# Pooled attention and squared-ReLU feed-forward on one core: all engine orders from an explicit table, and some loads and stores on ScalarE's DMA queue

## The chip, the cores and the metric

The kernel runs on one core of one Trainium2 chip. That core has TensorE (PE in the rows) for matrix products, VectorE (DVE), ScalarE (ACT) and GpSimd (POOL) for work on vectors, and SyncE (SP), which issues DMAs here. Each engine works through its own queue in order; semaphores join them. The metric is device time in microseconds (us), lower is better.

## The reference

Four batches of eight heads, 1152 keys of 64 numbers each. Queries are averaged in pairs, so a head has 576 of them. Attention over all keys is followed by a feed-forward layer with a squared ReLU on the 2304 x 512 result.

```python
q_pool = q.reshape(B, H, S // 2, 2, D).mean(axis=3)
scores = np.matmul(q_pool, k.transpose(0, 1, 3, 2)) / np.sqrt(D)
attn = np.exp(scores - scores.max(-1, keepdims=True))
attn = attn / (attn.sum(-1, keepdims=True) + 1e-09)
x = np.matmul(attn, v)          # then (b, s, h, d) -> (2304, 512)
r = np.maximum(x @ w_in, 0.0)   # 512 -> 2048
out = (r * r) @ w_out           # 2048 -> 512
```

All arrays are float32, and q and k come with a spread that makes scores large.

## The kernel before

The float32 products are made from float16 parts: a number is split into a high part and the low rest, and three products of parts are added. The work is a list of 2265 steps, each with a name, the engines that may do it, the steps that it depends on, and buffers that it takes and gives back. A name is two letters and numbers; these occur in the text:

- **Pairs of heads.** There are 16 (n = 0 to 15). Steps LK, LQ, LV load k, q, v of a pair into one of two `raw` buffers; KA and KD (and QA, QD, VA, VD) make the high and low parts; KT and QT transpose them by DMA into `kT` and `qT`; QX copies the halves of `qT` across partitions.
- **Chunks of 128 queries.** A pair has nine, 144 in all. S is the product with the keys, into one of two PSUM tiles `s`. MX (line 771, DVE) finds the row maximum, MB (line 778 on ACT, 781 elsewhere) finishes the bias, EX (line 795, ACT) takes the exponent. For chunks 36 to 143, HI (line 799 on ACT) casts the result to float16, LO (line 807) makes the low part, and TR (line 810) transposes both by DMA into `PT`. For chunks 0 to 35 (pairs 0 to 3) TP transposes on TensorE in float32 and TC (lines 846, 848) copies out. PV is the product with v, ED moves it out of PSUM.
- **Blocks of 256 rows.** There are nine of the feed-forward layer (j = 0 to 8). RV, RT, RU, RB and XR apply the softmax sums, XQ to XD scale and split the block; H (line 1119) and O (line 1168) are the two products in eight steps each; HA, G1, G2, G3 are the ReLU, its square and its split between them; OD and ST write the block out.
- **Weights.** w_in and w_out come through staging buffers (WL, UL, line 1222) and are turned into parts by W and U steps, of which W5 or U4, for instance, reads a staging buffer.

S of chunk i waits for EX of chunk i-2, because there are two `s` tiles. H, O, RB and other small products share two PSUM banks `ba` until the last EX; then six more (`bt`) open.

The method `Plan.order` decides engine and order. It simulates the list with fixed costs (`COST`, `Clock`), takes at each moment the step with the best priority (`off` and `off0` in `CFG`), and chooses among a step's engines by expected end. All DMAs are issued by `nc.sync`, that is by SyncE's queue, also QX of the pairs for which `CFG` says so.

Of the kernel before, what the change touches and what calls it, by code (L numbers as in the profile page):

```python
# [33 lines left out]
}  # L34


class Clock:


    W = 3413.3  # L40

    def __init__(self):
        self.warm, self.edge, self.used = False, self.W, 0.0

    def turn(self):
# [1413 lines left out]
```

## Time and profile before

| | us |
|---|---|
| median of three runs | 794.99 (794.79 to 800.12) |
| span of the profiled execution, first to last instruction | 794.4 |
| TensorE busy in it | 743.8 (94%) |
| VectorE busy | 571.4 (72%) |
| ScalarE busy | 589.7 (74%) |
| GpSimd busy | 350.1 (44%) |

The profiled execution has no time of its own beside its span; the span lies 0.6 us under the median of the runs. TensorE's busy time counts matrix products from start to modelled end, and at the lower of its two clock levels (1.2 and 2.4 GHz) the same product is busy twice as long. In a row, PEclk 1.00 is the higher level. Issuing a DMA isn't counted as busy.

### The profile page before, as it was taken

To read this page: it belongs to the slowest core of one execution; us is meant where nothing else is said; L and a number is where in the kernel's file an instruction comes from. 1 tells how busy PE (TensorE), PEld (TensorE's weight loads), DVE (VectorE), ACT (ScalarE), POOL (GpSimd) and SP (SyncE) were. 2 spreads that over 40 slices of the span, in tenths; PEclk is the share of its full clock that TensorE was granted. 3 is DMA by queue.
4 is the path that set the end of the run, shared out by engine and by line. 5 is a ranking of instruction groups with operands and counts; after the bars stand their busy time and mean duration, and the time that the engine had idled before them with its cause. 6 is when DMAs were issued, how large, how long until landed. Compare 5 with 4: busy or idle time off the path is not lost.

```text
span 794.4 us, 15338 instructions
## 1 busy us (share of the span) xinstructions
PE 743.8 (94%) x5998; PEld 491.7 (62%) x5998; DVE 571.4 (72%) x920; ACT 589.7 (74%) x874; POOL 350.1 (44%) x240
## 2 busy tenths in 40 slices
PE   5889888888999999979999999999999999999997
PEld 4665555555766676546756775577567657785654
DVE  4789987787789798787879888898898764202311
ACT  5776967899798798688987997899989864403512
POOL 2455421346686475544646575575366321001200
PEclk8899899999899999979999999999999999999999
DMA  8686573417889999999999999999999991000011
GB/s 325 225 233 187 167 204 106 120 31 142 168 172 199 194 225 218 219 206 215 186 212 199 217 208 207 202 228 195 209 217 191 173 183 25 1 2 13 14 27 28
DMA packets 324840, 128.96 MB, mean 162 GB/s; under 512 B 307104, under 2 KB 307872, under 8 KB 324768
## 3 DMA queue, kind: packets, MB, share of 16 engines
q1 hardware_dynamic: 324768, 127.98, 77.3%
q8 instruction: 47, 0.77, 0.4%
q14 instruction: 25, 0.20, 0.1%
HBM read 45.09 MB, written 4.72 MB: 63 GB/s over the span
## 4 chain that ended last, share of the span: by engine, by line
PE 78%; DVE 7%; ACT 5%; DMA 5%; issue 3%; SPq 1%; POOL 0%; DVEq 0%; ACTq 0%; POOLq 0%
PE ba L1168 17%; PE ba L1119 17%; PE s L760 12%; PE ba L955 10%; PE bt L1168 7%; PE bt L1119 6%; DVE s L771 3%; PE ba L836 3%; DMA region<-in_moe_w_in_dram 2%; PE ba L947 2%; ACT buf L795 2%; PE s L755 2%; DMA w<-in_moe_w_out_dram 2%; DVE PT L848 1%; ACT PT L846 1%
## 5 line engine op out<-in xcount | busy, mean ns | idle before, releaser
L771 DVE TENSOR_SCALAR_CACHE_REDUCE s<-s,esc 128x1152 f32<-128x1152 f32 x135 | 190.9, 1420 | 32.2 <-PE s L760 21.9
L1119 PEld LDWEIGHTS <-w 128*128 128x128 f16 x1728 | 169.4, 99 | 33.1 <-issue 7.0
L795 ACT ACTIVATE buf<-s,ca 128x1152 f32<-128x1152 f32 x144 | 174.4, 1212 | 14.2 <-DVE s L771 7.7
L807 POOL TENSOR_TENSOR buf<-buf,buf 128x1152 f16<-128x1152 f32 x53 | 130.9, 2472 | 54.1 <-ACT buf L799 44.2
L760 PE MATMUL s<-kT,qT 128*128 128x512 f16 x720 | 137.6, 330 | 9.3 <-ACT buf L795 9.0
L1168 PE MATMUL ba<-w,region 128*128 128x512 f16 x624 | 142.2, 379 | 1.3 <-ACT region L1129 0.7
L1168 PEld LDWEIGHTS <-region 128*128 128x128 f16 x864 | 82.8, 98 | 96.3 <-issue 2.5
L1119 PE MATMUL ba<-region,w 128*128 128x256 f16 x1104 | 128.7, 275 | 1.3 <-DVE x L1046 1.2
L799 ACT ACTIVATE buf<-buf 128x1152 f16<-128x1152 f32 x107 | 124.5, 1163 | 5.9 <-DMA PT<-buf 1.7
L760 PEld LDWEIGHTS <-qT 128*128 128x128 f16 x720 | 63.6, 100 | 66.9 <-issue 18.1
L807 DVE TENSOR_TENSOR buf<-buf,buf 128x1152 f16<-128x1152 f32 x55 | 77.1, 1404 | 14.4 <-ACT buf L799 14.1
L955 PE MATMUL ba<-PT,v 128*64 128x320 f16 (+1 forms) x1296 | 85.4, 290 | 0.0
L955 PEld LDWEIGHTS <-v 128*64 128x64 f16 x1296 | 70.8, 111 | 14.7 <-issue 7.1
L1146 POOL TENSOR_TENSOR region<-region 128x512 f16<-128x512 f32 x35 | 49.2, 1405 | 51.4 <-ACT region L1139 50.0
L1146 DVE TENSOR_TENSOR region<-region 128x512 f16<-128x512 f32 x37 | 29.1, 793 | 58.7 <-ACT region L1139 55.8
L836 PE MATMUL ba<-ident,buf 128*128 128x128 f32 x324 | 54.4, 296 | 14.8 <-ACT buf L795 5.5
L1134 ACT ACTIVATE region<-region 128x512 f16<-128x512 f32 x72 | 45.1, 626 | 20.3 <-PE bt L1168 17.3
L836 PEld LDWEIGHTS ba<-ident,buf 128*128 128x128 f32 x324 | 36.4, 148 | 30.7 <-ACT PT L846 8.7
L1168 PE MATMUL bt<-w,region 128*128 128x512 f16 x240 | 52.6, 379 | 0.0
L1142 POOL TENSOR_TENSOR region<-region 128x512 f32<-128x512 f32 x11 | 14.6, 1329 | 83.6 <-ACT region L1134 83.6
L846 ACT ACTIVATE PT<-ba 128x384 f32<-128x384 f32 x76 | 35.7, 490 | 18.6 <-PE ba L836 17.1
L1119 PE MATMUL bt<-region,w 128*128 128x256 f16 x432 | 48.7, 273 | 0.0
(189 smaller groups left out, 944.1 us busy)
## 6 DMA issues: line engine op xcount, KB each, us to landing
raw<-in_q_dram SPq DMA_DIRECT2D x32, 288.0 KB, 3.8
raw<-in_k_dram SPq DMA_DIRECT2D x15, 576.0 KB, 4.8
region<-in_moe_w_in_dram SPq DMA_DIRECT2D x8, 1024.0 KB, 6.2
w<-in_moe_w_out_dram SPq DMA_DIRECT2D x8, 1024.0 KB, 5.8
raw<-in_v_dram SPq DMA_DIRECT2D x12, 576.0 KB, 4.7
out_dram<-buf SPq DMA_DIRECT2D x22, 128.0 KB, 2.4
v<-in_v_dram SPq DMA_DIRECT2D x4, 576.0 KB, 6.2
out_dram<-half SPq DMA_DIRECT2D x14, 128.0 KB, 3.3
```

The costliest lines, as they stand in the source:

```text
L760: nc.tensor.matmul(s[:, x, :w], lhsT=qt[:, l].rearrange("p c m -> p (c m)")[:, 128 * c0 + h : 128 * c0 + h + 255 : 2], rhs=rhs, **st)
L771: nc.vector.tensor_scalar(st3(), st3(), sc, 3e38, op0=ALU.mult, op1=ALU.min, accum_out=a[:, x : x + 1])
L795: nc.scalar.activation(P(), st3(), AF.Exp, bias=a[:, 1:2], scale=s1, accum_out=col)
L799: nc.scalar.activation(hl()[:, 0], P(), AF.Copy)
L807: e.tensor_tensor(out=hl()[:, 1], in0=P(), in1=hl()[:, 0], op=ALU.subtract)
L836: nc.tensor.matmul(t[:, y], lhsT=P()[:, c * 128 : (c + 1) * 128], rhs=ident, is_transpose=True, start=(y == 0), stop=(y == 2), skip_group_ ...
L846: nc.scalar.activation(out, t, AF.Copy)
L955: nc.tensor.matmul(px[h * 64 : (h + 1) * 64, 64 * r * (1 - h) : 64 * r * (1 - h) + N], lhsT=vv[:, h, kc, vl, :], rhs=p2(vi, r, h, 9 * pl + ...
L1119: nc.tensor.matmul(ph[:, f2], lhsT=w16[0][:, SLOT[f // 4], wl, a, f % 4 * 128 : (f % 4 + 1) * 128], rhs=xhl()[:, xl, a], start=(i == 0), s ...
L1134: nc.scalar.activation(gt[u][:, 0], rt[u % 2], AF.Square)
L1146: e.tensor_tensor(out=gt[u][:, 1], in0=rt[u % 2], in1=gt[u][:, 0], op=ALU.subtract)
L1168: nc.tensor.matmul(p[:, :DM], lhsT=g[:, gl, f % 2, tt * 128 : (tt + 1) * 128], rhs=w16[1][:, SLOT[f // 4], wl, f % 4], start=(f == 0 and g ...
```

## The change

The simulation in `Plan.order`, its costs and its priorities go. In their place stands the string `ORDER`: three characters a step, which give the step's number, its engine and the buffer that it takes. The list of steps and their dependences stay. A sixth engine name, AQ, means a DMA issued by `nc.scalar`, that is ScalarE's queue; loads of pairs 4 to 15 and all stores may have it. The listing contains functions for another way to make the scores (`flipped`, `part`, `kz`), which are not used, since `FLIP` is empty in `CFG`.

```diff
+ORDER = (
+    "26W27W28W29X2C000W2E12DG2BO2G02F82I12H82K02MW2JG2LG81006W02803O82G01O2P18AG13W8382QG8408B904G86185807O"
...
-    ENG = ("PE", "ACT", "DVE", "POOL", "SP")
+    ENG = ("PE", "ACT", "DVE", "POOL", "SP", "AQ")
...
+        for k in range(0, len(ORDER), 3):
+            a, b, c = (DIGIT[x] for x in ORDER[k : k + 3])
+            i, e, x = 64 * a + b, self.ENG[c // 8], c % 8
             o = ops[i]
+            assert i not in gone and e in o["engs"] and all(self.at[d] in gone for d in o["deps"] + list(o["after"])), o["name"]
             o["eng"] = e
...
+            gone.add(i)
+            out.append(o)
...
+    def queue(o):
+        return nc.scalar if o["eng"] == "AQ" else nc.sync
...
+        def aq(cost):
+            return {"AQ": cost} if n >= NP else {}
...
-        def load_kv(t, src):
-            nc.sync.dma_start(
+        def load_kv(o, t, src):
+            queue(o).dma_start(
...
-                nc.sync.dma_start(out=raw("q", n)[h : h + 127 : 2], in_=sv[h])
+                queue(o).dma_start(out=raw("q", n)[h : h + 127 : 2], in_=sv[h])
...
-                add(("QX", n, z), {"SP": 850} if n in cfg("QXD", ()) else alt("QX", DVE=470, POOL=1500), [("QT", n)] + old, lambda o, z=z: qx(o, z), need)
+                add(("QX", n, z), {"DVE": 470, "POOL": 1290, "SP": 850}, [("QT", n)] + old, lambda o, z=z: qx(o, z), need)
...
-                    nc.sync.dma_start(out=ob[c], in_=t[z * 64 : (z + 1) * 64])
+                    queue(o).dma_start(out=ob[c], in_=t[z * 64 : (z + 1) * 64])
```

Counted by step, the engines change most for these (before, after). HI: ACT 107, 55; DVE 0, 29; POOL 1, 24. G2: ACT 59, 38; DVE 2, 15; POOL 11, 19. HA: ACT 47, 38; DVE 25, 34. MB: ACT 42, 48; DVE 20, 40; POOL 46, 20. KA: ACT 4, 11; POOL 11, 4. QX: DVE 12, 8; POOL 10, 5; SP 8, 17. To ScalarE's queue go 8 LK, 5 LQ, 10 LV and 7 ST, which are 42 DMAs, since LQ and ST are two each. TensorE does the same steps, and its order differs only by swaps of neighbours.

Three places follow, each of before and of the change apart. Line numbers differ between the two kernels; a row's tiles tell which step it is.

**ScalarE around chunks 71 to 74** (the change from block 1 to block 2). Rows with `sums` are EX, a cast from `buf` to `buf` is HI, the one from `region` to `buf` with 1024 columns is XQ of block 2, `psc` is KA or QA, `acc` is QQ, `ru` is RU, `xs` is XA, the one that writes `ca` is MB, `esc` is ED. Before:

```order
L578 ACTIVATE buf_93,acc<-raw_101 128x576
L795 ACTIVATE buf_94,sums_88<-s_113,ca 128x1152
L799 ACTIVATE buf_98<-buf_94 128x1152
L1058 ACTIVATE buf_96<-region 128x1024
L343 ACTIVATE buf_93<-raw_101,psc 128x9x64
L795 ACTIVATE buf_94,sums_85<-s_112,ca 128x1152
L799 ACTIVATE buf_96<-buf_94 128x1152
L1017 ACTIVATE ru<-ba_114 32x128
L795 ACTIVATE buf_95,sums_85<-s_113,ca 128x1152
L799 ACTIVATE buf_99<-buf_95 128x1152
L343 ACTIVATE region<-region,xs 128x1024
```

The same place after the change; L375 is the load LV of pair 9:

```order
L260 ACTIVATE buf_94<-raw_101,psc 128x9x64
L774 ACTIVATE buf_96,sums_88<-s_113,ca 128x1152
L260 ACTIVATE region<-ba_115,esc 128x256
L375 DMA raw_102<-in_v_dram 128x2x576
L774 ACTIVATE buf_98,sums_85<-s_112,ca 128x1152
L1041 ACTIVATE buf_95<-region 128x1024
L774 ACTIVATE buf_93,sums_85<-s_113,ca 128x1152
L1000 ACTIVATE ru<-ba_114 32x128
L778 ACTIVATE buf_95<-buf_93 128x1152
```

EX of chunk 72 (the first with `sums_85`) stood behind HI, XQ and QA, and now stands behind ED and a load; EX of chunk 73 stood behind HI and RU, and now stands behind XQ alone.

**VectorE at the first block steps** (XR of block 1, the row with `region` and `ba`, beside QX of pair 5). MX are the rows that write `s` and `ca`. Before:

```order
L771 TENSOR_SCALAR s_113,ca<-s_113,esc 128x1152
L807 TENSOR_TENSOR buf_94<-buf_96,buf_94 128x1152
L1046 TENSOR_TENSOR region<-region,ba_114 128x512
L655 COPY qT_106<-qT_106 64x1152
L771 TENSOR_SCALAR s_112,ca<-s_112,esc 128x1152
L1046 TENSOR_TENSOR region<-region,ba_115 128x512
```

The same place after the change, where L782 is HI:

```order
L750 TENSOR_SCALAR s_113,ca<-s_113,esc 128x1152
L760 TENSOR_SCALAR ca<-ca 128x1
L782 CAST buf_94<-buf_98 128x1152
L786 TENSOR_TENSOR buf_94<-buf_98,buf_94 128x1152
...
L750 TENSOR_SCALAR s_113,ca<-s_113,esc 128x1152
L1029 TENSOR_TENSOR region<-region,ba_115 128x512 x2
```

The copy of `qT` between the two XR steps is gone from VectorE (SyncE issues it), and a cast that ScalarE did has come.

**SyncE's queue from the second pair's transposes on** (L652 is QX as a DMA, L1222 the weights). Before:

```order
L455 DMA raw_102<-in_k_dram 128x2x576
L652 DMA qT_106<-qT_106 64x1152 x2
L1222 DMA region<-in_moe_w_in_dram 128x2x1024
L633 DMA_TRANSPOSE kT_104<-buf_99 128x18x128
L1222 DMA region<-in_moe_w_in_dram 128x2x1024
```

After the change:

```order
L375 DMA raw_102<-in_k_dram 128x2x576
L1205 DMA region<-in_moe_w_in_dram 128x2x1024
L565 DMA_TRANSPOSE kT_104<-buf_99 128x18x128
L383 DMA raw_101<-in_q_dram 64x1152 x2
L1205 DMA region<-in_moe_w_in_dram 128x2x1024
```

The two QX of pair 1 no longer stand ahead of the weights on this queue.

## Rows read from the trace of the kernel before

**Rows 1.** Busy time by engine in stretches of the span (count), clock, DMA share.

```profile
0.00:182.09 182.09, 149.95 (x1148) 99.72 (x1149) 145.15 (x248) 140.52 (x214) 72.40 (x50) 0.94 0.57 174
182.09:204.98 22.89, 19.21 (x140) 12.55 (x140) 15.04 (x24) 17.77 (x24) 13.76 (x8) 0.85 0.96 179
198.15:204.98 6.83, 5.67 (x26) 3.78 (x26) 4.09 (x10) 2.62 (x5) 3.71 (x4) 0.50 1.09 208
204.98:338.51 133.53, 132.53 (x1109) 86.20 (x1107) 111.17 (x165) 112.61 (x165) 84.98 (x56) 1.00 1.06 199
338.51:368.82 30.31, 23.41 (x186) 14.29 (x185) 26.38 (x51) 25.56 (x37) 16.26 (x13) 0.77 1.06 212
344.92:355.16 10.24, 7.28 (x37) 3.50 (x38) 8.74 (x23) 8.62 (x13) 7.97 (x6) 0.50 1.11 231
...
368.82:642.30 273.48, 271.27 (x2319) 181.16 (x2318) 233.91 (x361) 239.87 (x354) 150.09 (x103) 1.00 1.08 203
642.30:789.80 147.50, 147.47 (x1105) 97.80 (x1103) 38.91 (x73) 53.33 (x83) 12.65 (x11) 1.00 0.14 29
789.80:794.40 4.60, 0.00 (x0) 0.00 (x0) 0.81 (x1) 0.00 (x0) 0.00 (x0) 0.75 0.38 88
```

**Rows 2.** Groups by line: busy us, mean ns of one, idle before.

```profile
L771 DVE TENSOR_SCALAR_CACHE_REDUCE s<-s,esc 128x1152 f32<-128x1152 f32 x135 | 190.9, 1420 | 32.2 <-PE s L760 21.9 <-PE s L755 7.3 <-ACT region L343 1.2
L795 ACT ACTIVATE buf<-s,ca 128x1152 f32<-128x1152 f32 x144 | 174.4, 1212 | 14.2 <-DVE s L771 7.7 <-POOL ca L781 2.9 <-DMA PT<-buf 2.3
...
L799 ACT ACTIVATE buf<-buf 128x1152 f16<-128x1152 f32 x107 | 124.5, 1163 | 5.9 <-DMA PT<-buf 1.7
```

**Rows 3.** The chain that ended last: start, us, what.

```profile
43.56 5.89 DMA region<-in_moe_w_in_dram
...
189.74 6.99 DMA qT<-half
...
206.26 2.62 PE ba L1119 x24
```

**Rows 4.** Timeline of SyncE's queue.

```profile
42.23 1.16 SPq L652 DMA_DIRECT2D qT<-qT  x2
43.56 1.08 SPq L1222 DMA_DIRECT2D region<-in_moe_w_in_dram  x1
```

**Rows 5.** Timeline of VectorE and TensorE at block 0's third H step.

```profile
196.75 0.46 DVE L655 COPY qT<-qT 64x1152 f16<-64x1152 f16 x1 [2.12 <-DMA qT<-half]
...
198.58 0.68 DVE L1046 TENSOR_TENSOR region<-region,ba 128x512 f32<-128x512 f32 x1
...
199.31 5.28 PE L1119 MATMUL ba<-buf,w 128*128 128x256 f16 x24 [3.68 <-DVE region L1046]
```

**Rows 6.** Timeline of TensorE and ScalarE, chunks 72 to 74.

```profile
346.33 2.08 PE L760 MATMUL s<-kT,qT 128*128 128x512 f16 x6 [2.26 <-ACT buf L795]
...
342.36 1.06 ACT L1058 ACTIVATE buf<-region 128x1024 bf16<-128x1024 f32 x1 [0.17 <-DVE region L1046]
344.30 0.77 ACT L343 ACTIVATE buf<-raw,psc 128x576 f16<-128x576 f32 x1 [0.89 <-DVE psc L602]
344.98 1.20 ACT L795 ACTIVATE buf<-s,ca 128x1152 f32<-128x1152 f32 x1
...
348.66 0.27 ACT L1017 ACTIVATE ru<-ba 32x128 f16<-32x128 f32 x1 [1.19 <-PE ba L1012]
348.83 1.20 ACT L795 ACTIVATE buf<-s,ca 128x1152 f32<-128x1152 f32 x1
```

**Rows 7.** Single lines: duration ns minimum/median/maximum, first and last start.

```profile
L655 DVE COPY qT<-qT x12: 453/733/2532, 196.8 to 595.3; 64x1152 f16<-64x1152 f16 x12
...
L1146 DVE TENSOR_TENSOR region<-region x37: 679/691/2892, 187.3 to 781.4; 128x512 f16<-128x512 f32 x37
...
L810 SPq DMA_TRANSPOSE PT<-buf x108: 2400/2840/5931, 191.1 to 652.0; - x108
...
L455 SPq DMA_DIRECT2D raw<-in_k_dram x15: 368/579/1435, 7.4 to 555.8; - x15
```

**Rows 8.** Timeline of GpSimd and VectorE at 185 to 190.

```profile
185.55 4.10 POOL L1347 TENSOR_TENSOR w<-region,w 128x2048 f16<-128x2048 f32 x1 [2.41 <-ACT region L1343]
...
187.31 2.89 DVE L1146 TENSOR_TENSOR region<-region 128x512 f16<-128x512 f32 x1 [1.86 <-ACT region L1139]
```

More of the change, by code (lines that the diff above doesn't have):

```diff
@@ L95, in add @@
         self.ops.append(
[L96 removed]
+            dict(name=name, engs=engs, deps=[d for d in deps if d], emit=emit, take=take, give=give, after=after)
         )
     def order(self, last):
[L100 to L110 removed]
@@ L111, in order @@
-        free = dict.fromkeys(self.ENG, 0.0)
-        port = {"DVE": 0.0, "POOL": 0.0}
-        ready = {e: set() for e in self.ENG}
-        end, start = [0.0] * n, [0.0] * n
-        avail = [0.0] * n
-        dma = [0.0, 0.0]
-        pe = Clock()
-        last = self.at[last]
-        slack = {e: cfg("sl" + e, x) for e, x in self.SLACK.items()}
-        pen, bl = cfg("pen", 1000), cfg("bl", 0.5)
-        slots, held = self.slots, {}
-        def at_least(o):
-            if not o["take"]:
-                return 0.0
-            _, rs, rest = o["take"]
-            f = sorted(x for r in rs for x in slots[r] if x is not None)
-            return f[rest] if len(f) > rest else None
@@ L176, in order @@
             if o["take"]:
                 key, rs, _ = o["take"]
-                f, r, x = min((f, r, x) for r in rs for x, f in enumerate(slots[r]) if f is not None)
-                slots[r][x] = None
+                r, x = [(r, y) for r in rs for y in range(len(self.slots[r]))][x]
+                assert self.slots[r][x] is not None, key
+                self.slots[r][x] = None
                 held[key] = self.slot[key] = (r, x)
-            start[i] = s
-            if e == "SP":
-                x = max(s + 1700, dma[0])
-                dma[0] = end[i] = x + cost
-                free[e] = max(s + 550, end[i] - 2500)
-            elif e == "PE":
-                free[e] = end[i] = s + pe.run(s, cost)
-            else:
-                s2 = s
-                if e == "POOL":
-                    s2 = max(s, port["DVE"])
-                elif e == "DVE" and o["name"][0] in self.LOCK:
-                    s2 = max(s, port["POOL"])
-                free[e] = end[i] = s2 + cost
-                if e == "POOL" or e == "DVE" and o["name"][0] in self.LOCK:
-                    port[e] = end[i]
@@ L197, in order @@
             if o["give"]:
                 r, x = held.pop(o["give"])
-                slots[r][x] = end[i] + self.LAT[e]
-            out.append((s, len(out), i))
+                self.slots[r][x] = 0.0
             if i == last:
-                slots["t"] = [end[i] + 200] * len(slots["t"])
-            for u in later[i]:
-                left[u] -= 1
-                if not left[u]:
-                    enable(u)
-            for u in users[i]:
-                left[u] -= 1
-                same = e == "PE" and "PE" in ops[u]["engs"]
-                avail[u] = max(avail[u], end[i] + (5 if same else self.LAT[e]))
-                if not left[u]:
-                    enable(u)
@@ L213, in order @@
[L213 to L219 removed]
[5 rows of a table removed]
[L225 removed]
+                self.slots["t"] = [0.0] * len(self.slots["t"])
+            gone.add(i)
@@ L818, in chunk @@
                 add(("S", i), {"PE": 2200 if len(both(i)) == 2 else 2050}, [("KC", n, x) for x in range(3)] + [("QC", n, z) for z in range(2)] + back, scores4, i)
+        elif n in flip_:
+            if both(i)[0] == i:
+                back = [("EX", y - 2) for y in both(i)]
+                add(("S", i), {"PE": 1665 if len(both(i)) == 2 else 1115}, [("KT", n), ("QX", n, 0), ("QX", n, 1)] + back, flipped, i)
         else:
@@ L1367 @@
     lastr = {}
-    for n, pair, js in first + [(p, p, ORD) for p in range(NP, B * NP)]:
+    for n, pair, js in first + [(p, p, ORDF if p in flip_ else ORD) for p in range(NP, B * NP)]:
         p = preps[n]
```

244 lines of the change are left out of this document (135 added, 109 removed), and 11 rows, old and new, of tables (COST, DEF).

## The prediction

> **What bounds the kernel now.** The first view is the busy time of each engine in stretches of the span, cut where TensorE's behaviour changes [rows 1]. From 204.98 to 338.51, from 368.82 to 642.30 and from 642.30 to 789.80 us TensorE is busy all but 1.0, 2.2 and 0.0 us, at the high clock. There the sum of its products sets the time, and no other engine's order can shorten it. TensorE idles in three places. Up to 182.09, where block 0's first H starts, it is idle 182.09 - 149.95 = 32.1 us. From 182.09 to 204.98 it is idle 22.89 - 19.21 = 3.7 us, and the 5.67 us of busy time from 198.15 to 204.98 run at PEclk 0.50, so 2.8 of them come from the low level. From 338.51 to 368.82 it is idle 30.31 - 23.41 = 6.9 us, and of the 7.28 busy us at PEclk 0.50 (344.92 to 355.16) 3.6 come from the low level; a shorter stretch at that level follows and is left as a reserve. After 789.80 comes the last store, 4.6 us. So what a new order can win lies in 32.1 + 6.5 + 10.5 us; the rest is TensorE at work.
>
> The second view is the groups by line [rows 2]: a chunk costs VectorE 1.42 us for MX, and ScalarE 1.21 for EX plus 1.16 for HI. The third is the chain that ended last; where it leaves TensorE it names a load of weights and a transposing DMA into qT [rows 3]. The fourth is the timeline at those places.
>
> **The change, part by part.** TensorE gets the same steps. Its 743.8 us at these clocks stay, except where the low level goes.
>
> *Up to 182.09.* On SyncE's queue the two QX of pair 1 (42.23, 1.16 us) were issued ahead of a load of w_in at 43.56 [rows 4], which the chain then follows for 5.89 us [rows 3]. In the new order they aren't on that queue, so this load can go out up to 43.56 - 42.23 = 1.3 us earlier, more if QX's own wait held the queue, and nothing if the staging buffer is free only then. Beyond that, engine loads hardly change: up to block 0's first H, ScalarE takes over eight TC and one EX and gives away ED, QC and UA, and VectorE the reverse, all within 4 us. What remains is order. VectorE is busy 145.15 of 182.09 us, 80%; where TensorE is full it reaches 233.91 of 273.48, 86% [rows 1]. At that share its work would take 169.7 us, 12.4 less. That is the far end of the gain; finer interleaving of TP steps through two banks could as well cost something, for which I allow 6 us, half the gain's end. I take 5 us less: the load's 1.3, and a third of the remaining 11.
>
> *182.09 to 204.98.* VectorE held XR of block 1 behind a QX copy that waited 2.12 us for its DMA; XR ended at 199.26, and H started at 199.31 after 3.68 us idle [rows 5]. The chain calls the cause the 6.99 us of that DMA [rows 3]. The change takes this copy off VectorE, and both XR follow each other. What is late next is the MX ahead of them, 1.42 us, which starts when S of chunk 41 is done; an H step of 2.62 us [rows 3] in front covers it. Of 3.7 + 2.8 us I take 5.
>
> *338.51 to 368.82.* There are no block steps here until H of block 2, so TensorE runs at the pace of S, MX, EX, S. EX of chunk 72 started at 344.98 behind XQ and QA, which waited for other engines until 342.36 and 344.30, and TensorE's next S waited 2.26 us for it; EX of chunk 73 at 348.83 stood behind HI and RU [rows 6]. In the new order both EX are ahead of these. From EX of chunk 72 to EX of chunk 74, ScalarE also loses one HI of 1.16 us, and further casts up to chunk 77. Against it stands a load issued by ScalarE just ahead of EX 72: 0.58 us by SyncE's median for this form [rows 7]. Of 6.9 + 3.6 us I take 6.
>
> *The casts.* From 182 to 642, 52 HI leave ScalarE, 60.5 us by 1.163 [rows 2]. About 28 go to VectorE, for which no row shows a cast of this shape. The near rows are the copy of half as many bytes of f16, at best 0.45 us, and MX over the same 1152 columns, 1.42. I take 0.8, nearer to the copy since both run from SBUF. Then VectorE has 15.04 + 111.17 + 26.38 + 233.91 = 386.5 us there [rows 1], plus 28 x 0.8 = 22, plus ten G3 at 0.69 [rows 7] = 7; its other swaps cancel to a microsecond or two. That is 416 of about 449 us, 93%. At 1.42 it would be 433, 97%. TensorE's full stretches have been seen beside 86% only, so I charge 2 us of new stalls; the ends are 0 and 10.
>
> A GpSimd step can also hold VectorE: G3 took 2.89 us instead of 0.69 while WD ran on GpSimd, and ended when that did, at 190.2 against 189.65 [rows 8]; QX copies range from 0.45 to 2.53 us [rows 7]. The Trainium skill, in "SBUF — State Buffer", section "Who interferes with whom", says that a VectorE cast may take a port pair that it shares with GpSimd, and that whichever comes second then waits for the other's whole instruction. The trace agrees for G3; it has no cast to show. By that rule some of the 28 casts would wait up to the 2.5 us of an LO on GpSimd, and an estimate by that rule takes the end of 10 us, which makes the sum 788.
>
> *The DMAs on ScalarE.* Some 30 of the 42 fall between 182 and 642. At 0.58 us they are 17 us of ScalarE's time. It has 17.77 + 112.61 + 25.56 + 239.87 = 395.8 us there; less 60.5, plus 17, that is 353 of 449, 79% instead of 86%. So their cost is hidden if each costs what it costs SyncE. What queues behind a load on ScalarE is mostly EX, and S two chunks later waits for that. For SyncE, nine more QX (0.58 each as a DMA) stand against 42 DMAs less, so its queue, 108 transposing issues of 2.84 [rows 7] and the loads, gets lighter by some 19 us; nobody on the full stretches waits for it.
>
> **Sum.** 794.4 - 5 - 5 - 6 + 2 = 780.4 in the profiled execution; the median lies 0.6 above the span, so 781.
>
> **The rivals.** *ScalarE's issues hold up EX (slower).* A load on ScalarE would cost more than 0.58 us if it has to wait while SyncE issues a transposing DMA, 2.84 us at the median and up to 5.93 [rows 7], which is most of the time in the full stretches. Then each costs some 3.4 us, and EX behind it starts that much later. TensorE has usually one block step of 2.62 us between two S, so an issue decides from about 2.6 us on. About 23 loading and storing steps stand in this stage; if each exposes one microsecond, counting S and EX of the other tile as the rest of the cover, that is +23: 781 + 23 = 804. For it speaks that SyncE's queue is seldom at rest there; against it, that the same form has a median of 0.58 and a minimum of 0.37 us on SyncE, among transposing issues. The Trainium skill, in "Perfetto Trace Analysis", section "DMA Instruction — HWDGE (DVE, Sync)", has a lock under which the descriptor generator serves one issuing queue at a time. No run here shows two queues; by that page the result would be this rival's.
>
> *The stalls come back elsewhere (no change).* VectorE is the most loaded engine after the change. With casts at 1.42 us it is at 97%, and MX, which S and EX need, comes late in the full stretches; +10 there instead of +2, and nothing won up to 182.09, gives 794.4 - 11 + 10 = 793.4, or 794 as a median. For it speaks that no stretch shows TensorE full beside so busy a VectorE; against it, that LO, QX and G3 can wait while MX goes first.
>
> *The change doesn't do what it says*: a load on ScalarE lands no sooner than on SyncE, since no load is waited for in the full stretches. That changes no term above, which take nothing for earlier loads but the one of w_in, so the time would be 781 too.
>
> **How the numbers follow.** Forecast, 766 to 787: 0.63. Stalls elsewhere, 787 to 803: 0.22. ScalarE's issues, 803 to 820: 0.13. Better than 766, if all of 12.4 + 6.5 + 10.5 is won (765 in the span): 0.02. The range 766 to 800 leaves out the better end, nearly all of the slower rival and a little of the one between. A measurement of this kernel can tell about 1%, that is 8 us, from no change: faster than 787 gets 0.65, slower than 803 gets 0.13, between 0.22.
>
> **What would show it.** In the changed kernel's stretches: H of block 0 starts near 177; no idle of 3 us before its third step; S of chunks 72 to 77 wait less than 2 us in total, and PEclk stays at 1.00 there; TensorE is still full from then to the end. Casts on VectorE have a minimum near 0.7 and a median under 1 us. DMA issues on ScalarE have a median of 0.6; if it is 3 and EX is what TensorE waits for, the slower rival holds. The prediction is wrong if H of block 0 starts later than 182, or if the full stretches show more than 5 us of idle time.

## The result, and the profile after

The changed kernel takes 806.18 us (median of 4 runs, 803.27 to 811.34) beside 795.97 for the kernel before on the same chip. The ratio is 1.0115 with an interval from 1.0068 to 1.0162: it is slower by about 1.2%. The profiled execution took 803.27, with a span of 801.5 against 794.4. Further down, medians are over all runs of a kernel, while ratios leave out its few slow ones (one of four in h1, one of twelve in j1, two of twelve in j2).

The busy time by engine in stretches of the changed kernel, to be held against [rows 1]; columns as there. Block 0's first H starts at 168.58.

```profile
0.00:168.58 168.58, 145.03 (x1153) 95.25 (x1154) 144.10 (x249) 140.62 (x215) 67.14 (x51) 0.98 0.62 185
168.58:181.53 12.95, 12.95 (x108) 8.58 (x107) 7.31 (x13) 11.36 (x18) 8.12 (x7) 1.00 0.74 127
181.53:192.42 10.89, 4.58 (x24) 3.32 (x23) 6.70 (x10) 3.16 (x5) 4.93 (x2) 0.69 1.09 212
192.42:325.42 133.00, 126.52 (x1043) 82.18 (x1041) 104.73 (x179) 95.10 (x151) 59.05 (x39) 1.00 1.02 192
325.42:350.00 24.58, 16.41 (x140) 9.46 (x141) 16.59 (x33) 14.19 (x21) 13.84 (x10) 0.86 1.16 221
350.00:460.00 110.00, 102.76 (x914) 70.59 (x909) 92.63 (x156) 82.27 (x139) 50.27 (x32) 1.00 1.08 203
460.00:640.00 180.00, 173.76 (x1465) 115.47 (x1465) 147.66 (x242) 126.01 (x202) 84.12 (x62) 0.99 1.04 195
640.00:796.80 156.80, 156.80 (x1167) 102.38 (x1162) 56.60 (x106) 42.27 (x69) 28.82 (x26) 1.00 0.21 41
```

Span less TensorE's busy time gives its idle time, stretch by stretch. Up to the first H it is 168.58 - 145.03 = 23.6 us, where it was 32.1. From there to 192.42 it is 6.3, all in one stall (3.7 before, up to 204.98). From 192.42 to 640 it is 6.5 + 8.2 + 7.2 + 6.2 = 28.1 us; before, from 204.98 to 642.30, it was 1.0 + 6.9 + 2.2 = 10.1. After 640 it is 0 in both, with 4.7 and 4.6 for the last store. TensorE's busy time falls from 743.8 to 738.8, since less of the first part runs at PEclk 0.50 (6.8 us of it, 20.5 before). Together: -8.5 + 2.6 + 18.0 + 0.1 - 5.0 = +7.2, the 7.1 us by which the span grew. So the early part won 13.5 us (182.09 to 168.58), and the stretches that had been full gave back 18 and more.

What ended TensorE's idle time in the stage, after: groups by line from 192 to 645 us (name, shapes, count | busy, mean ns | idle before, by what ended it).

```profile
L1102 PE MATMUL ba<-region,w 128*128 128x256 f16 x960 | 111.5, 275 | 3.0 <-ACT region L1112 2.9 <-DVE region L1029 0.2
L696 PE MATMUL s<-kT,qT 128*128 128x512 f16 x526 | 99.5, 330 | 7.7 <-ACT buf L774 7.5
L938 PE MATMUL ba<-PT,v 128*64 128x320 f16 (+1 forms) x1188 | 77.9, 287 | 2.8 <-DMA PT<-buf 2.8
L511 PE MATMUL ba<-acc,cols 128*128 128x2 f32 (+1 forms) x40 | 6.8, 239 | 11.5 <-ACT buf L498 7.9 <-DVE region L1029 1.8 <-ACT half L498 1.5
```

The same view of the kernel before has 5.6 us at S and 0.8 at GF:

```profile
L760 PE MATMUL s<-kT,qT 128*128 128x512 f16 x552 | 105.7, 331 | 5.6 <-ACT buf L795 5.6
L591 PE MATMUL ba<-acc,cols 128*128 128x1 f32 (+1 forms) x42 | 6.6, 226 | 0.8 <-DVE region L1046 0.8
```

GF, the small product that sums the squares of a loaded pair (L511), is the new place of waiting: 11.5 us, most of it for ScalarE's squares (L498). The view of waits for ScalarE in the same window, after, tells what ScalarE stood for (total us, times, longest):

```profile
ACT buf L774 <- DMA PT<-buf: 18.2, 10, 4.0
ACT buf L778 <- DMA PT<-buf: 12.0, 7, 5.1
```

and before:

```profile
ACT buf L795 <- DMA PT<-buf: 2.3, 2, 1.4
ACT buf L799 <- DMA PT<-buf: 1.7, 2, 1.0
```

EX (L774) and HI (L778) each write into a buffer of the ring of seven, and a buffer that holds a chunk for its transposing DMA is free only when that has landed. These waits rose from 4.0 to 30.2 us. The timeline of the largest stall, at 325 us, shows the whole path (rows of ScalarE, of SyncE and of TensorE):

```profile
306.46 0.38 ACTq L375 DMA_DIRECT2D raw<-in_v_dram  x1
309.19 0.37 ACTq L375 DMA_DIRECT2D raw<-in_k_dram  x1
...
319.97 1.16 ACT L778 ACTIVATE buf<-buf 128x1152 f16<-128x1152 f32 x1 [5.10 <-DMA PT<-buf]
320.10 1.27 ACTq L383 DMA_DIRECT2D raw<-in_q_dram  x2
...
326.78 1.22 ACT L774 ACTIVATE buf<-s,ca 128x1152 f32<-128x1152 f32 x1 [3.45 <-DMA PT<-buf]
...
329.20 1.20 ACT L774 ACTIVATE buf<-s,ca 128x1152 f32<-128x1152 f32 x1
...
330.39 0.67 ACT L498 ACTIVATE buf<-raw 128x576 bf16<-128x576 f32 x1
...
307.84 4.35 SPq L789 DMA_TRANSPOSE PT<-buf  x1
312.28 7.48 SPq L565 DMA_TRANSPOSE kT<-buf  x1
319.93 6.70 SPq L789 DMA_TRANSPOSE PT<-buf  x2
...
331.21 0.58 PE L511 MATMUL ba<-acc,cols 128*128 128x2 f32 x2 [5.79 <-ACT buf L498]
```

Two loads of 576 KB go out within 3 us. The transpose issued at 307.84 lands only at 319.88, 12.0 us later (median here 5.5), and SyncE needs 7.48 us to issue the next one, for kT. ScalarE's HI waits 5.10 us for the first, its EX 3.45 for another, the square of Q stands behind both, and TensorE idles 5.79 us before GF; PEclk then falls to 0.50 for 6.8 us.

TensorE also comes to this GF earlier than before. The text on the change says that its order differs only by swaps of neighbours; the two lists of steps show more: 397 of TensorE's 511 steps stand at another place in its sequence, the farthest 23 places off. This GF, of pair 9, stood behind S of chunk 73 and now stands ahead of S of chunk 71. That alone doesn't make the stall: S of chunk 71, next in line, needs EX of chunk 69 (the row at 329.20), which ends at 330.40, 0.8 us before GF runs. No run changed TensorE's order by itself, so what its moves cost or gain is not shown; below, "order" includes it.

VectorE meets the same thing at 183 us, where one of its new casts waits 6.88 us for a kT transpose to land, with GF's scales and an MX queued behind it:

```profile
183.13 2.80 DVE L782 CAST buf<-buf 128x1152 f16<-128x1152 f32 x1 [6.88 <-DMA kT<-buf]
...
187.84 5.00 PE L1102 MATMUL ba<-buf,w 128*128 128x256 f16 x24 [6.31 <-DVE psc L521]
```

VectorE's load grew less than forecast. From 181.53 to 640 us it is busy 368.3 of 458.5 us, 80%, and over the whole span 577.1 us beside 571.4, though it has 29 casts more (25.9 us). The main saving is in KD, QD and VD, the low parts of k, q and v: 69 steps in either kernel, 87.9 us before and 57.8 after, with the shortest of them unchanged at 0.80 us. Why the others became shorter no run isolates. The largest group of them, before and after:

```profile
L374 DVE SCALAR_TENSOR_TENSOR buf<-raw,psc,buf 128x576 f16<-128x576 f32 x34 | 44.1, 1306 | 0.0
L291 DVE SCALAR_TENSOR_TENSOR buf<-raw,psc,buf 128x576 f16<-128x576 f32 x33 | 28.1, 863 | 0.3 <-POOL buf L262 0.3
```

Last, the single lines that the prediction named (ns minimum/median/maximum, first and last start):

```profile
L782 DVE CAST buf<-buf x29: 743/755/2799, 171.8 to 652.8; 128x1152 f16<-128x1152 f32 x29
L375 ACTq DMA_DIRECT2D raw<-in_v_dram x10: 369/375/445, 172.0 to 595.5; - x10
L383 ACTq DMA_DIRECT2D raw<-in_q_dram x10: 479/584/748, 245.1 to 443.8; - x10
L789 SPq DMA_TRANSPOSE PT<-buf x108: 2381/2850/5487, 182.1 to 681.9; - x108
```

### The profile page after: what moved, and what is told of

Its sections match the earlier page's. It is cut to its first block, busy times and chain, and to the rows that moved or that the text cites. A ratio compares the mean times of both kernels' runs of the same rounds, so it can differ in the third digit from the quotient of the medians.

```text
span 801.5 us, 15240 instructions
## 1 busy us (share of the span) xinstructions
PE 738.8 (92%) x5998; PEld 487.2 (61%) x5998; DVE 577.1 (72%) x986; ACT 515.0 (64%) x816; POOL 316.3 (39%) x223
## 5 line engine op out<-in xcount | busy, mean ns | idle before, releaser
L774 ACT ACTIVATE buf<-s,ca 128x1152 f32<-128x1152 f32 x144 | 175.3, 1218 | 63.8 <-POOL ca L760 20.3
L1102 PEld LDWEIGHTS <-w 128*128 128x128 f16 x1728 | 169.4, 99 | 36.5 <-issue 11.1
L786 POOL TENSOR_TENSOR buf<-buf,buf 128x1152 f16<-128x1152 f32 x50 | 122.8, 2457 | 119.5 <-ACT buf L778 63.2
L1151 PE MATMUL ba<-w,region 128*128 128x512 f16 x672 | 153.4, 379 | 0.2 <-DVE region L1114 0.2
L786 DVE TENSOR_TENSOR buf<-buf,buf 128x1152 f16<-128x1152 f32 x58 | 80.0, 1386 | 4.2 <-ACT buf L778 3.9
L938 PEld LDWEIGHTS <-v 128*64 128x64 f16 x1296 | 70.5, 110 | 17.2 <-issue 5.9
L778 ACT ACTIVATE buf<-buf 128x1152 f16<-128x1152 f32 x55 | 63.4, 1156 | 13.9 <-DMA PT<-buf 12.0
L1129 POOL TENSOR_TENSOR region<-region 128x512 f16<-128x512 f32 x32 | 38.4, 1207 | 78.9 <-ACT region L1122 41.1
L1125 POOL TENSOR_TENSOR region<-region 128x512 f32<-128x512 f32 x19 | 20.7, 1088 | 86.5 <-ACT region L1117 86.3
L285 POOL TENSOR_SCALAR buf<-buf,cols 128x1152 f16<-128x1152 f32 x24 | 31.4, 1310 | 45.2 <-ACT buf L774 29.1
L829 ACT ACTIVATE PT<-ba 128x384 f32<-128x384 f32 x83 | 38.5, 497 | 13.7 <-PE ba L819 13.3
```

The costliest lines, as they stand in the source:

```text
L774: nc.scalar.activation(P(), st3(), AF.Exp, bias=a[:, 1:2], scale=s1, accum_out=col)
L778: nc.scalar.activation(hl()[:, 0], P(), AF.Copy)
L786: e.tensor_tensor(out=hl()[:, 1], in0=P(), in1=hl()[:, 0], op=ALU.subtract)
L829: nc.scalar.activation(out, t, AF.Copy)
L938: nc.tensor.matmul(px[h * 64 : (h + 1) * 64, 64 * r * (1 - h) : 64 * r * (1 - h) + N], lhsT=vv[:, h, PERM[h][kc] if n in flip_ else kc, vl ...
L1102: nc.tensor.matmul(ph[:, f2], lhsT=w16[0][:, SLOT[f // 4], wl, a, f % 4 * 128 : (f % 4 + 1) * 128], rhs=xhl()[:, xl, a], start=(i == 0), s ...
```

## The experiments

Both kernels have the same 2265 steps with the same needs, so the order of before can be written as a table too, and tables can be cut and mixed; the buffer numbers are then given out anew where they must be. In the edits below, `new` and `old` are the two orders as lists of steps. "Before" is the kernel before, run beside each. Idle is span less TensorE's busy time in the profiled run; it is 50.6 us in the kernel before and 62.7 in the changed one.

| run | median | before | ratio, interval | idle |
|---|---|---|---|---|
| e1_all_on_sp | 809.62 | 799.25 | 1.0135 (1.0088 to 1.0182) | 62.6 |
| e2_only_queue | 800.26 | 799.25 | 1.0027 (0.9991 to 1.0062) | 55.4 |
| e3_new_then_old | 786.02 | 799.25 | 0.985 (0.9779 to 0.992) | 47.1 |
| e4_old_then_new | 825.66 | 799.25 | 1.0344 (1.028 to 1.0409) | 72.0 |
| f1_casts_back | 869.58 | 797.62 | 1.0901 (1.0862 to 1.094) | 106.5 |
| f2_casts_moved | 813.45 | 797.62 | 1.0199 (1.0184 to 1.0214) | 64.6 |
| f5_new_engines | 849.13 | 797.62 | 1.0645 (1.0621 to 1.067) | 89.0 |
| f6_old_engines | 868.94 | 797.62 | 1.0895 (1.0859 to 1.0931) | 102.3 |
| g1_chain_close | 898.59 | 798.13 | 1.1249 (1.121 to 1.1288) | 126.0 |
| g1b_chain_close_new_engines | 896.91 | 798.13 | 1.121 (1.1168 to 1.1252) | 133.8 |
| g2b_chain_far | 949.6 | 798.13 | 1.1897 (1.1863 to 1.1932) | 166.6 |
| h1_half_loads | 786.59 | 798.13 | 0.9813 (0.9748 to 0.9878) | 50.7 |
| h2_half_loads_before | 796.46 | 797.15 | 1.0003 (0.998 to 1.0027) | 53.6 |
| f3_qx_back | 809.7 | 797.15 | 1.0172 (1.0115 to 1.0229) | 70.5 |
| k1_cut_at_74 | 795.19 | 797.15 | 0.9982 (0.9946 to 1.0018) | 53.3 |
| k2_cut_at_100 | 803.28 | 797.15 | 1.0067 (1.0038 to 1.0097) | 63.0 |
| j1_eight_buffers | 799.71 | 796.96 | 1.003 (0.9998 to 1.0062) | 57.6 |
| j2_seven_control | 806.15 | 796.96 | 1.0095 (1.0059 to 1.013) | 63.6 |

### The queue, and the two halves of the order

Three theories stood at the start. A: the new orders of the later stretches do it. B: loads issued behind ScalarE's work come late. C: the DMA engines are full from 205 to 640 us and would eat any head start.

**e1_all_on_sp**

```diff
-        return nc.scalar if o["eng"] == "AQ" else nc.sync
+        return nc.sync
```

> The changed kernel, with its 30 plain loads and stores issued by SyncE again, each at its place in the table; every order stays. Theory A (the new orders of the later stretches feed the transposes late): the queue has little to do with it, 802 to 810 us. Theory B (loads behind ScalarE's work come late and hold up the squares and GF): the gain of the first 180 us stays, 785 to 795. Theory C (the DMA engines are full from 205 to 640 us in either kernel, so a head start is lost whatever is done): 800 to 806, within 1% of the changed kernel.

**e2_only_queue** (30 steps, 42 DMAs)

```diff
-ORDER = new
+ORDER = [(s, "AQ") if new puts s on "AQ" else s for s in old]
```

> The kernel before in its own order on every engine, but with the same 30 loads and stores issued by ScalarE where SyncE had them. Theory A: near the kernel before, 793 to 799. Theory B: slower, 801 to 810, with idle of TensorE before GF that ScalarE's squares end. Theory C: no change, 794 to 797, since the same bytes pass the same engines.

**e3_new_then_old**

```diff
-ORDER = new
+ORDER = new[:610] + [s for s in old if s not in new[:610]]
```

> The table of the changed kernel up to the first H of block 0 (610 of 2265 steps), then the order of the kernel before for all that is left, all loads there by SyncE but for what the first part has. Theory A: the first third's gain of 12 to 14 us is kept, 780 to 784. Theory B: the same, 780 to 784, if no load of ScalarE's queue is left in the later part. Theory C: the gain is lost between 205 and 640 us, 790 to 796.

**e4_old_then_new**

```diff
-ORDER = new
+ORDER = old[:609] + [s for s in new if s not in old[:609]]
```

> The order of the kernel before up to the first H of block 0 (609 steps), then the table of the changed kernel. Theory A: the later stretches cost 20 to 24 us more without the early gain, 814 to 820. Theory B: the same. Theory C: with the start 13 us later the DMA engines are as full as in either kernel, and the time is 804 to 809, as changed.

Undoing the queue leaves the time where it was, and the queue alone changes nothing that can be told apart. B falls. The two cuts point the same way: the new first third keeps 13 us when the old order follows it, and the old first third with the new order behind it costs 26 us. Both lie on A's side, though past its ranges (786 for 780 to 784, 826 for 814 to 820). C in its plain form falls with e3, which moves the same loads and transposes and yet keeps its lead. The stretches of e3 (the cut is at 168.58):

```profile
0.00:168.58 168.58, 144.15 (x1146) 95.90 (x1147) 142.44 (x248) 139.23 (x215) 66.44 (x51) 0.99 0.62 185
...
192.00:645.00 453.00, 439.99 (x3729) 288.58 (x3728) 381.03 (x592) 384.56 (x565) 252.53 (x172) 0.99 1.07 202
```

Its idle time in the 453 us is 13.0; the kernel before has 13.8 in the same window. ScalarE's waits for a transposed buffer, in e3:

```profile
ACT buf L778 <- DMA PT<-buf: 0.9, 2, 0.5
```

and in e4:

```profile
ACT buf L774 <- DMA PT<-buf: 20.3, 10, 3.9
ACT buf L778 <- DMA PT<-buf: 11.2, 7, 5.2
```

So e3 beats both kernels, by 1.5% (0.8 to 2.2) against the one before. No better version was found.

### Engines against places

In the order of before, HI follows EX directly on ScalarE in 106 of 107 chunks; in the new one in 17 of 55, with other steps between elsewhere, and HI is on another engine in 53. When each EX is paired with its LO and its transpose (92 and 89 chunks between 195 and 600 us, means), LO starts 1.7 us after EX ends before, and 5.5 after the change; the chunk is transposed 13.8 and 17.5 us after EX. The next seven runs asked whether it is the engines (A1), the places (A2), or the distance of HI, LO and TR from EX (A3).

**f1_casts_back**

```diff
-..., EX(i) on ACT, ..., HI(i) on DVE or POOL, ...
+..., EX(i) on ACT, HI(i) on ACT, ...
```

> The changed kernel, with the 53 casts HI that its table gives to VectorE and GpSimd run by ScalarE again, each right behind the EX of its chunk; all else as changed. In the runs so far the way from the end of EX to the start of LO takes 1.7 us a chunk in the order of before and 5.5 in the new one. Theory A1 (the casts wait in the other engines' queues, the ring of seven buffers runs short, and EX and the squares wait): the way falls to 2 or 3 us, and the time to 790 to 798. Theory A2 (the places of the steps in the order do it, whichever engine runs the cast; ScalarE has 60 us more to do): the way stays over 4 us, 803 to 812.

**f2_casts_moved**

```diff
-ORDER = new
+ORDER = [(s, engine of s in new) if s is HI else s for s in old]
```

> The kernel before, with its casts HI on the engines that the changed kernel gives them (53 of 108 off ScalarE), each at its old place in the program; nothing else moved. Theory A1: the way from EX to LO rises to 3 us or more, and the time to 802 to 810. Theory A2: under 2.5 us, 793 to 799.

**f5_new_engines**

```diff
-ORDER = new
+ORDER = [(s, engine of s in new, SP for AQ) for s in old]
```

> The order of the kernel before, with every step on the engine that the changed kernel gives it (casts, differences, merges, copies, activations, QX), each at its old place in the program, loads and stores by SyncE. Theory A1: slower than before by 8 us or more, 803 to 815. Theory A2: within 1% of before, 790 to 800.

**f6_old_engines**

```diff
-ORDER = new
+ORDER = [(s, engine of s in old) for s in new]
```

> The order of the changed kernel, with every step on the engine that the kernel before gives it, at its new place in the program, loads and stores by SyncE. Theory A1: the later stretches lose their waits and the early gain stays, 785 to 797. Theory A2: 803 to 815, as changed or worse.

**g1_chain_close** (g1b keeps the engines of `new`, g2b exchanges `old` and `new` and keeps the engines of `old`)

```diff
-ORDER = new
+ORDER = new with HI, LO, TR of a chunk at place(EX in new) + place(s in old) - place(EX in old), engines of old
```

> The changed table, in which the cast HI, the difference LO and the transpose TR of each chunk from the 37th on stand as many steps behind the chunk's EX as in the order of before (4, 9 and 28 steps in the mean, against 10, 20 and 37 in the changed table), on the engines that they have before; all else as changed. Theory A3 (in the new order a chunk's probabilities stay longer in the ring of seven buffers, so that EX, HI and behind them the squares wait for a transpose to land): the way from EX to LO falls from 5.5 to under 3 us, ScalarE's waits for a transposed buffer from 30 to under 10 us, and the time to 786 to 797. Rival (the new order stalls for other reasons, GF and the squares by their own places): 800 to 815.

> The same as g1, with HI and LO on the engines of the changed table. Theory A3: the places decide, 788 to 800, within 6 us of g1. Rival (VectorE and GpSimd are what makes the casts late): 803 to 815.

> The order of the kernel before, in which HI, LO and TR stand as far behind EX as in the changed table (10, 20 and 37 steps in the mean), each on its engine of before; all else as before. Theory A3: slower than before by 10 us or more, 806 to 830, with the way from EX to LO over 4 us and the waits of ScalarE for a transposed buffer over 15 us. Rival: within 1% of before, 790 to 802.

Each mixture is slower than both of its parents, and than the kernel before by 2% (f2) to 19% (g2b); none of the seven falls in a range that was named for it. f2 and f5 move the way that A1 says, and past its ranges (the way from EX to LO rises only to 2.1 and 2.2 us); f1 and f6 go against it. A3's forecast fails in g1: the way from EX to LO does become short there (2.7 us), and yet the run takes 899 us. That doesn't refute A3, since the moved steps stop other queues. The view of waits of g1, from 192 to 645 us, shows why a shorter way doesn't pay by itself:

```profile
POOL buf L786 <- ACT buf L778: 163.3, 28, 16.0
DVE buf L786 <- ACT buf L778: 42.7, 20, 8.5
```

LO now stands at the head of GpSimd's and VectorE's queues before ScalarE has come to its HI, and holds up what is behind it. In f2 it is MX that comes late behind the casts on VectorE; GpSimd's merges wait 42.5 us for it, where they waited 35.1 before, and ScalarE's 36.5, where they waited 19.5:

```profile
POOL ca L760 <- DVE s L750: 42.5, 25, 6.0
ACT ca L757 <- DVE s L750: 36.5, 23, 3.8
```

So an order and its engines belong together, and runs that move one kind of step through a whole table say little on what that kind costs in either.

### Transfers that land late

Theory D: only the new order stands and waits where a transfer lands late; the old one has room there.

**h1_half_loads** (and **h2_half_loads_before**, the same on `old`)

```diff
-                out=t.rearrange("p h c d -> p h (c d)"),
-                in_=src[b, 2 * hp : 2 * hp + 2].rearrange("h (p c) d -> p h (c d)", c=9),
+                out=t.rearrange("p h c d -> p h (c d)")[:, : 2 if n < NP else 1],
+                in_=src[b, 2 * hp : 2 * hp + (2 if n < NP else 1)].rearrange("h (p c) d -> p h (c d)", c=9),
...
-            for h in range(2):
+            for h in range(2 if n < NP else 1):
```

> The changed kernel, with only the first of two heads of Q, K and V loaded from the fifth pair on (the other half of each buffer keeps older data): some 8 to 9 MB of the 89 MB between 192 and 645 us are left out. Theory C (the DMA engines are full there and set the pace): faster by 10 us or more, 780 to 796. Theory A3: the transposes land a little sooner, the places stay; 800 to 807.

> The order of the kernel before, with the same loads halved as in the run that took the changed kernel from 806 to 787 us. Theory C (the DMA engines, full from 205 to 640 us, set the pace of either kernel): faster by as much, 775 to 783. Theory D (only the new order stands and waits where a transpose or a load lands late; the old one has room there): 791 to 797.

**f3_qx_back**

```diff
-ORDER = new
+ORDER = [(s, engine of s in old) if s is QX else s for s in new]
```

> The changed kernel, with QX run by the engines that run it before (VectorE and GpSimd for the later pairs), so that 12 copies of 144 KB less pass the DMA engines between 192 and 645 us. If these copies are what delays the transposes: 794 to 801. If not (theory D lies in the other steps' places): 802 to 812.

**k1_cut_at_74** and **k2_cut_at_100**

```diff
-ORDER = new
+ORDER = new up to EX(74) + the rest of old        # k2: EX(100)
```

> The changed table up to EX of chunk 74 (some 350 us), then the order of before. By the work that TensorE has done at a time, the changed kernel is 15 us ahead at 320 us and 1 to 8 us ahead from 340 to 440. Theory D (the lead is lost at a few places of the new order, the first at 325 us): 785 to 791, between the cut at 168 us (786 us) and the changed kernel. If the whole loss comes after 350 us: 778 to 784.

> The changed table up to EX of chunk 100 (some 470 us), then the order of before. At that time the changed kernel's lead is down to 2 us. Theory D: 791 to 798, near the kernel before. If the loss lies in the later stretches or in how the two orders fit together: under 788 or over 802.

Halving the loads takes 20 us from the changed kernel (806 to 787; 24 by the ratios, 1.0115 to 0.9813) and nothing from the kernel before. That agrees with D, and it is against what h1 alone had seemed to say for C. Both runs also leave out twelve issues, since a pair's Q comes by one load instead of two, so bytes and issues are not told apart. The QX copies that were moved to the DMA engines have no part in it: with them back on VectorE and GpSimd the time is 810. The cuts show where the loss comes: 786 with the new order up to 168 us, 795 up to 350, 803 up to 470, 806 with all of it. These medians come from several chips; by the ratios (0.985, 0.9982, 1.0067, 1.0115) it is some 10 us between 168 and 350, 7 between 350 and 470, and 4 after that, the last within the noise. So it is not one accident. Both k1 and k2 lie above what D had named for them (785 to 791, 791 to 798), and what the joint of the two orders costs is in each of the cuts. The window of h1 has 81.82 MB instead of 89.48, and these waits of ScalarE:

```profile
ACT buf L774 <- DMA PT<-buf: 10.1, 6, 5.1
ACT buf L778 <- DMA PT<-buf: 7.7, 7, 2.2
```

They fell from 30.2 to 17.8 us.

### The ring of buffers

**j1_eight_buffers** and its control **j2_seven_control** (the control only gives out the buffers by the same rule)

```diff
-    NBUF, NRAW = 7, 2
+    NBUF, NRAW = 8, 2
...
-        "half": [buf_p.tile([128, 1152], F16, name="half0")],
+        "half": [],
...
-    xmt = x_p.tile([128, NP, TB], F32, name="xm")
+    xmt = x_p.tile([128, NP, TB], F16, name="xm")
```

> The changed kernel's orders and engines, with a ring of eight buffers where it has seven and one of half the size (the room comes from the ninth block's x, kept in 16 bits); each step takes the free buffer that was given back first. In the changed kernel ScalarE stands for 30 us at EX and HI until a transpose has landed and its buffer is free (4 us before the change). Theory D by the ring (the new orders hold buffers longer, so that a late landing stops ScalarE, and behind it the squares and GF): those waits fall under 12 us and the time to 785 to 798, below its control by 8 us or more. Rival (the new order loses it by other waits, the ring being only where they show): within 5 us of the control.

> The control of the run with eight buffers: the changed kernel with its seven buffers and the half one, each step taking the free buffer that was given back first; only the numbers of the buffers differ from the changed kernel. By either theory 802 to 812 us, since the steps and their order are the same.

The eighth buffer is worth 6.4 us by the medians and 5.2 by the ratios, between the two theories' numbers, and ScalarE's waits do not fall under 12 us. In j1:

```profile
ACT buf L774 <- DMA PT<-buf: 12.5, 9, 3.2
ACT buf L778 <- DMA PT<-buf: 8.9, 4, 3.7
```

In j2 (23.7 us, where the changed kernel, which takes the same time, has 30.2):

```profile
ACT buf L778 <- DMA PT<-buf: 13.4, 6, 3.4
ACT buf L774 <- DMA PT<-buf: 10.3, 4, 4.2
```

Between 170 and 205 us j1 has no stall of TensorE over 0.8 us, where its control has one of 4.3 and the changed kernel one of 6.3; that is most of the 6.0 us by which its idle time is less. GF still costs it 9.1 us of idle time (7.8 in the control). So one more buffer gives back a quarter to a third of the some 20 us that lie between e3 and the control; what more buffers would give is not shown.

## Why the prediction was wrong, point by point

The forecast was 781 (766 to 800); the time is 806, and the sign is wrong. By its steps, in the profiled execution:

- *Up to 182.09*, -5 taken, bounds -12.4 to +6. The mechanism was right and the size too small: -13.5, past the bound. Idle time fell by 8.5 us and busy time by 4.9, as PEclk went from 0.94 to 0.98; the bound had counted order alone and left TensorE's clock out. VectorE is busy 144.10 of 168.58 us, 85%, close to the 86% that the bound was drawn from. The load of w_in went out at 39.75 instead of 43.56.
- *182.09 to 204.98*, -5 taken. The copy that held XR is gone from VectorE, but a cast took its place, with a longer wait (6.88 us for a DMA instead of the 2.12 of [rows 5]), and the stall is 6.3 us instead of 3.7. The prediction asked what is late next on VectorE and looked only at MX; the steps that were moved onto that queue at the same place were not gone through.
- *338.51 to 368.82*, -6 taken. S of chunks 72 to 77 waits less than 1 us, as said. Only EX of chunk 72 came ahead of XQ, though; EX of chunk 73 still stands behind it, as the rows of the change show. And a stall appears ahead of this place, at 325 us, with 5.79 us at GF and 6.8 us at the low clock.
- *New stalls in the full stretches*, +2 taken, bounds 0 to 10. This is the step that failed. Idle time there rose from 10.1 to 28.1 us, which with the 6 us that should have gone is some +24. The term was drawn from VectorE's load alone. VectorE is no bound: its casts take 0.755 us at the median (0.8 was assumed), and it is busy at most 84% of these stretches, 368 us in all where the prediction had 416. That its other swaps cancel was wrong, since KD, QD and VD became 30 us shorter. The sentence that led astray is "nobody on the full stretches waits for it", said of SyncE's queue. It was true of the old order, where ScalarE waited 4.0 us in all for a transposed buffer, and was carried over to a new one whose whole point is that steps stand elsewhere; there it waited 30.2. h1 and h2 show the difference: with half the loads the new order gets 20 us back, the old one nothing.
- *ScalarE's issues hold up EX*, the slower rival. Its 804 is near the result and its mechanism is not what happened: issues on ScalarE take 0.375 us (V) and 0.584 (Q) at the median, and e1 and e2 show no price of the queue. Two loads of Q took 1.27 us to issue at 320.10, while SyncE was issuing transposes from 319.93 to 326.63. The rule of the Trainium skill in "Perfetto Trace Analysis", section "DMA Instruction — HWDGE (DVE, Sync)", that one issuing queue is served at a time, shows in no median of the issue times by more than 0.05 us (Q in e2: 0.636 on ScalarE, 0.587 on SyncE), though both queues run together.
- *VectorE as the bound* is refuted by the same 84%. The port rule of "SBUF — State Buffer", section "Who interferes with whom", in the Trainium skill, agrees with the casts' longest time of 2.80 us: that cast started at 183.13, while a GpSimd step of 4.06 us was running, and ended at 185.93, 0.6 us after it. At a median of 0.755 such a wait is rare.

What is shown: the loss belongs to the table after the first third (order and engines together, TensorE's order among them), it is spread from 168 to 470 us, it needs full-sized loads, and neither the queue nor the QX copies make it. What the traces show but no run has isolated: that it passes through EX and HI waiting for transposed buffers, and through the squares behind them to GF. Which steps would have to be moved to take it away stays open; the bulk moves (f and g) could not tell, since they broke more than they mended.

## What to carry to other kernels

A stretch where TensorE is full says that the other queues have room in that order, and a new order must earn that room again: when all orders change, price each full stretch by what the new order puts in front of each step on the other queues, above all steps that take a buffer which a DMA gives back. Test a new order in two halves: cutting the tables at one point, both ways, told more here than any change to one kind of step, and one of the two halves was the best kernel. When a stage seems bound by its transfers, lighten them in both versions; only the difference between the two says whether it is the transfers or the waiting for them.

## What was not expected of the hardware

Plain loads on a second queue issue as fast as on the first, but land later: Q 4.8 us at the median from ScalarE's queue and 3.4 from SyncE's in the same kernel, between 192 and 645 us. e2 has 4.8 and 3.6, and takes the time of the kernel before. One transpose among two 576 KB loads took 12.0 us to land, where the longest was 8.4 before. And a DMA share above 1.0 in both kernels was no sign that transfers set the pace: with 82.93 MB instead of 91.59 MB in the window, the kernel before took the same time.
